# A transformer layer on one core: the same operations in another written-out order, with VectorE's additions of the means to the query weights set between operations of GpSimd

## The chip, the core and the metric

The kernel runs on one core of a Trainium2 chip. The metric is the device time of one execution in microseconds (us). The core has five engines that run their own instruction streams and wait for each other by semaphores: TensorE (PE in the profile, with its weight loads as PEld), VectorE (DVE), ScalarE (ACT), GpSimd (POOL) and SyncE (SP), which here only issues DMAs.

## The reference

One layer over 2048 rows of width 640: a linear attention of 32 heads of 20, then a gated product of two projections, both behind a layer norm and with a residual.

```python
def _A_ref(x, wqkv, w_phi, wo):
    qkv = (x @ wqkv) ...                      # q, k, v: 32 heads of 20
    pq = einsum("bhsd,hdf->bhsf", q, w_phi)
    pk = einsum("bhsd,hdf->bhsf", k, w_phi)
    phi_q = concatenate([softmax(pq), softmax(-pq)], axis=-1)
    phi_k = concatenate([softmax(pk), softmax(-pk)], axis=-1)
    kv = einsum("bhsf,bhsd->bhfd", phi_k, v)
    z  = einsum("bhsf->bhf", phi_k)
    num = einsum("bhqf,bhfd->bhqd", phi_q, kv)
    den = einsum("bhqf,bhf->bhq", phi_q, z) + 1e-6
    return (num / den) @ wo

def _B_ref(x, w_gate, w_up, w_down):
    return ((x @ w_gate) * (x @ w_up)) @ w_down

h = x + _A_ref(layernorm(x), A_wqkv, A_w_phi, A_wo)
h2 = h + _B_ref(layernorm(h), B_w_gate, B_w_up, B_w_down)
```

## The kernel before

The rows are worked on as 16 tiles of 128 (number T below), the widths as 5 chunks of 128. The layer norm's scale is applied behind the projections, its mean is folded into the weights, and w_phi is folded into the key and query weights, so that one projection gives the scores. Every step is recorded as an operation that belongs to a named unit; a unit may have operations on several engines:

- warm, wk, x0 to x4, wv, c0 to c4, wm, y0 to y4: preparation of the weights. x and y are rounds of TensorE that fold w_phi into the key and query weights, each evacuated by ScalarE (even numbers) or VectorE (odd). wk, wv and wm hold the sums over the weights; c subtracts the means from the value weights.
- **wq0 to wq4** (lines 744 to 755): add the mean (negative, nmeanq) to one chunk of the turned query weights, in place, 128x640 bf16. wq1 and wq3 are on ScalarE (L751), wq0, wq2 and wq4 on VectorE (L754, a tensor_scalar from SBUF to SBUF). Rounds y need all five.
- s0, s2, s4, s8, s12: layer norm statistics of two or four tiles: matmuls, a few reads by VectorE (L620, L624), then a chain of small operations on GpSimd that ends in the scales rs and nrs and, when there is time, the means mv (L640).
- **kT** (keys): a projection (10 matmuls of 320 columns; L579 is the helper that issues all matmuls), the largest absolute score by VectorE (L847), its product with the scale, called nb (L850), and two exponentials on ScalarE (L855) that read the projection's PSUM buffer. **KT** normalises them: sums (L869) and their reciprocals (L871) on VectorE, then one product over 128x1280 on GpSimd (L872).
- vT (values): a projection and one scaled copy by ScalarE (L878).
- **qT, QT** (queries): as kT and KT, with the sums at L909 and the reciprocals at L915 on VectorE, two products on GpSimd (L916, L921), and two transposing DMAs (L476).
- A0 to A14: the attention sums over two tiles each, one operation for each of two PSUM banks, 10 and 12 matmuls of 63 columns. A14 needs the last K. Aout: VectorE reads each bank with two operations (L959, L962) into KV. Everything after it needs KV.
- nT (numerator over denominator), hT (output projection, residual, statistics, turned by DMA or TensorE), fB.F.J (gate and up product of chunk F for four-tile block B), dT and eT (down projection and output).
- in, l..., t...: loads and transposing loads on SP. lx0 to lx3 each load four tiles of x.

There are 4 PSUM buffers of two banks (pool p_ps), 3 for the exponentials of queries, 2 each for the small sums and reciprocals. A unit that takes a buffer waits for whoever read it last. A projection holds its buffer until ScalarE's last exponential or copy of it.

The order of the operations on each engine is written out in the table ORDER: for each engine a list of units, where each mention takes the unit's next operation on that engine. `place()` walks through these lists, gives out the buffers, and `finish()` sets the semaphore waits. So an edit of ORDER moves operations, and with them the choice of buffers and the waits, but adds and removes no work.

```python
g.op("DVE", lambda e, a=a: e.tensor_scalar(out=WT[:, 0, a, :], in0=WT[:, 0, a, :], scalar1=nmeanq[:, a:a + 1], scalar2=None,
                                           op0=ALU.add), t=0.34, lat=0.46, rd=[R_nmu, R_WT[0][a]], wr=[R_WT[0][a]])
...
g.op("POOL", lambda e: e.tensor_tensor(out=x, in0=x, in1=Rk[:, vr.i, :].unsqueeze(2).to_broadcast([P, 2 * H, DH]), op=ALU.mult),
     rd=vr.R + R_phik[t], wr=R_phik[t], use=[vr], t=2.33)
```

The t and lat in the code are the author's estimates for the planner.

Of the kernel before, what the change touches and what calls it, by code (L numbers as in the profile page):

```python
# [61 lines left out]

ORDER = {
# [14 lines left out]
    "DVE":  # L78
# [11 lines left out]
    "ACT":  # L90
# [9 lines left out]
    "POOL":  # L100
# [10 lines left out]
}  # L111

# [1059 lines left out]
```

## Time and profile before

| | us |
|---|---|
| three runs | 280.05, 280.16, 280.05; median 280.05 |
| the profiled execution | 279.95 |
| its span, first to last instruction | 278.0 |
| granted clock of TensorE | 1.00 |
| first matmul; start of the last one | 0.8; 275.0 |

The profile is of one execution. In a timeline a row is: start, duration, engine, line, operation, output and inputs by the program's names (buffer numbers left out), size, count of merged instructions, and in brackets the idle time before it with what ended it. Matmul ends are modelled; the next run of matmuls starts a little before the modelled end of the last. By name, ps is PSUM, phik holds the key exponentials and later the product of gate and up, Phi later holds KV, phiqT holds the query weights at first (Wnat, WT) and later the turned query exponentials.

### The profile page before, as it was taken

Reading aid. Unit: us, or ns where it says so; the run is one execution under the profiler, and the core shown is the slowest. Engines: PE = TensorE matmul, PEld = TensorE weight load, DVE = VectorE, ACT = ScalarE, POOL = GpSimd, SP = SyncE. Lnnn points to the kernel's source line nnn. Section 1 sums busy time; section 2 is a strip of 40 time slices with the busy share of each in tenths; the row PEclk is TensorE's granted clock in tenths of the full one; section 3 lists DMA queues with packets and bytes.
Section 4 is the critical chain, followed back from the end, with each engine's and each line's share of the span. In section 5 each row is a group of like instructions: output and inputs, shape, how many; then the busy total and the mean of one; then the engine's idle time right before and its main releaser. Section 6 shows DMA issues by size and latency. Waiting matters only on the chain.

```text
span 278.0 us, 5602 instructions
## 1 busy us (share of the span) xinstructions
PE 272.8 (98%) x2271; PEld 185.3 (67%) x2271; DVE 167.8 (60%) x314; ACT 140.8 (51%) x249; POOL 107.7 (39%) x152
## 2 busy tenths in 40 slices
PE   8999999999899999999999999999999999999996
PEld 8877677778778888877744556554566444457773
DVE  1999999999999887787737637353400123142012
ACT  3468989999576945445267344324114232131330
POOL 5527989899832404034440401502305110000430
PEclk9999999999999999999999999999999999999999
DMA  8998899106176889738660165505111000001112
GB/s 197 276 144 211 124 320 400 66 2 96 30 91 120 173 246 189 149 72 120 127 129 2 36 133 74 106 2 118 47 26 47 0 26 0 0 0 50 47 48 72
DMA packets 67241, 28.60 MB, mean 103 GB/s; under 512 B 57744, under 2 KB 65936, under 8 KB 67216
## 3 DMA queue, kind: packets, MB, share of 16 engines
q1 hardware_dynamic: 66288, 27.90, 45.2%
q10 hardware_dynamic: 928, 0.35, 0.5%
q8 instruction: 18, 0.29, 0.5%
q14 instruction: 7, 0.06, 0.1%
HBM read 11.82 MB, written 2.62 MB: 52 GB/s over the span
## 4 chain that ended last, share of the span: by engine, by line
PE 88%; DVE 7%; DMA 2%; SPq 1%; issue 1%; ACT 1%
PE ps L579 87%; DVE Ssum L869 2%; DMA Wp<-in_A_wqkv_dram 2%; DVE ps L847 1%; DVE Sq L909 1%; SPq L476 1%; DVE Rk L871 1%; ACT phik L855 1%; DVE phiqT L754 1%; PE ps L487 0%; DVE outb L1077 0%; SPq L472 0%; DVE t L624 0%; DVE Phi L959 0%; DVE rq L915 0%
## 5 line engine op out<-in xcount | busy, mean ns | idle before, releaser
L579 PE MATMUL ps<-phik,Wgu 128*128 128x512 bf16 (+1 forms) x600 | 107.8, 336 | 0.0
L579 PEld LDWEIGHTS ps<-phik,Wgu 128*128 128x128 bf16 x600 | 58.1, 98 | 42.5 <-DVE phik L1036 0.6
L1036 DVE TENSOR_TENSOR phik<-ps,gate 128x512 bf16<-128x512 f32 (+1 forms) x60 | 34.4, 581 | 62.2 <-PE ps L579 60.3
L579 PE MATMUL ps<-Wp,xT 128*128 128x320 bf16 (+1 forms) x480 | 69.3, 299 | 0.5 <-ACT phik L855 0.5
L1034 ACT ACTIVATE gate<-ps 128x512 bf16<-128x512 f32 (+1 forms) x60 | 30.3, 511 | 63.5 <-PE ps L579 50.8
L579 PE MATMUL ps<-vaug,phik 128*128 128x320 bf16 (+3 forms) x560 | 59.3, 265 | 0.0
L579 PEld LDWEIGHTS ps<-Wp,xT 128*128 128x128 bf16 x480 | 45.7, 98 | 18.2 <-ACT phik L855 0.7
L579 PEld LDWEIGHTS ps<-vaug,phik 128*128 128x128 bf16 x560 | 42.8, 98 | 16.4 <-DVE phik L1036 0.2
L1052 POOL TENSOR_TENSOR outb<-t,x_all 128x640 bf16<-128x640 f32 x12 | 16.8, 1397 | 70.5 <-ACT t L1049 55.4
L872 POOL TENSOR_TENSOR phik<-phik,Rk 128x1280 bf16<-128x1280 bf16 x16 | 37.7, 2366 | 4.6 <-DVE Rk L871 4.3
L1049 ACT ACTIVATE t<-ps,mh,rs 128x640 f32<-128x640 f32 x12 | 10.6, 883 | 33.4 <-PE ps L579 33.4
L847 DVE TENSOR_REDUCE ps<-ps 128x1 f32<-128x640 f32 (+1 forms) x32 | 26.4, 826 | 1.8 <-PE ps L579 1.4
L909 DVE TENSOR_REDUCE Sq<-eq 128x66 f32<-128x1320 bf16 x16 | 24.1, 1513 | 1.4 <-ACT eq L855 1.4
L869 DVE TENSOR_REDUCE Ssum<-phik 128x64 f32<-128x1280 bf16 x16 | 23.6, 1473 | 0.1
L916 POOL TENSOR_TENSOR rq<-Sq,rq 128x33 f32<-128x33 f32 x16 | 4.1, 255 | 46.4 <-DVE rq L915 42.4
L921 POOL TENSOR_TENSOR eq<-eq,rq 128x660 bf16<-128x660 bf16 x16 | 20.9, 1305 | 1.0
L855 ACT ACTIVATE eq<-ps,nb,rs 128x300 bf16<-128x300 f32 (+2 forms) x26 | 17.0, 688 | 6.1 <-DVE nb L850 5.9
L572 ACT ACTIVATE junk<-x_all 128x640 bf16<-128x640 bf16 x20 | 14.8, 738 | 9.5 <-DVE x_all L1013 9.4
L855 ACT ACTIVATE eq<-ps,nb,nrs 128x300 bf16<-128x300 f32 (+2 forms) x26 | 17.3, 692 | 0.0
L855 ACT ACTIVATE phik<-ps,nb,rs 128x640 bf16<-128x640 f32 x16 | 14.3, 891 | 3.2 <-DVE nb L850 3.0
L1013 DVE SCALAR_TENSOR_TENSOR x_all<-ps,mh,x_all 128x640 bf16<-128x640 f32 x16 | 14.1, 883 | 0.7
L855 ACT ACTIVATE phik<-ps,nb,nrs 128x640 bf16<-128x640 f32 x16 | 14.3, 896 | 0.0
(86 smaller groups left out, 225.0 us busy)
## 6 DMA issues: line engine op xcount, KB each, us to landing
x_all<-in_A_x_dram SPq DMA_DIRECT2D x4, 640.0 KB, 4.8
out_dram<-outb SPq DMA_DIRECT2D x15, 160.0 KB, 1.8
Wgu<-in_B_w_gate_dram SPq DMA_DIRECT2D x1, 1920.0 KB, 10.5
Wgu<-in_B_w_up_dram SPq DMA_DIRECT2D x1, 1920.0 KB, 16.0
vaug<-in_B_w_down_dram SPq DMA_DIRECT2D x1, 1920.0 KB, 9.6
Wp<-in_A_wqkv_dram SPq DMA_DIRECT2D x1, 800.0 KB, 5.0
phiqT<-in_A_wqkv_dram SPq DMA_DIRECT2D x1, 800.0 KB, 6.5
Wo<-in_A_wo_dram SPq DMA_DIRECT2D x1, 800.0 KB, 6.2
```

The source lines that it names most:

```text
L572: g.op("ACT", lambda e: e.activation(out=junk[:, v.i, :], in_=in_, func=func, accum_out=acc), rd=rd, wr=wr, use=[v], t=0.73, lat=0.97)
L579: ins = e.matmul(o_, lhsT=l_, rhs=r_, start=s_, stop=p_, skip_group_check=True)
L847: g.op("DVE", lambda e: e.tensor_reduce(out=mx(), in_=src(), axis=AX.XY if len(src().shape) == 3 else AX.X, op=ALU.max, apply_absolute_val ...
L855: g.op("ACT", lambda e, s=s, sc=sc, to=to, of=of: e.activation(out=to(s), in_=of(), func=ACT.Exp, bias=nb[:, i:i + 1], scale=sc[:, t:t + 1 ...
L869: g.op("DVE", lambda e: e.tensor_reduce(out=Ssum[:, vs.i, :], in_=x, axis=AX.X, op=ALU.add), rd=R_phik[t], wr=vs.R, use=[vs], t=1.39, lat=1.5)
L872: g.op("POOL", lambda e: e.tensor_tensor(out=x, in0=x, in1=Rk[:, vr.i, :].unsqueeze(2).to_broadcast([P, 2 * H, DH]), op=ALU.mult), rd=vr.R ...
L909: g.op("DVE", lambda e: e.tensor_reduce(out=Sq[:, vs.i, :].rearrange("p (w g) -> p w g", w=NQ), in_=feat(0, NQ).rearrange("p w (g f) -> p ...
L921: return e.tensor_tensor(out=x, in0=x, in1=rq[:, vr.i, :].rearrange("p (w h) -> p w h", h=HW).unsqueeze(3).to_broadcast([P, NQ, HW, DH]), ...
L1013: g.op("DVE", lambda e: e.scalar_tensor_tensor(out=xv, in0=PS[v.i][:, :, 0:HALF], scalar=mh[:, t:t + 1], in1=xv, op0=ALU.subtract, op1=ALU ...
L1034: g.op("ACT", lambda e: e.activation(out=gate[:, vg.i, 0:P * n], in_=PS[v.i][:, 0, 0:P * n], func=ACT.Copy), rd=[v.R[0]], wr=vg.R, use=[v, ...
L1036: g.op("DVE", lambda e: e.tensor_tensor(out=hhT[:, hb, ft, sl], in0=PS[v.i][:, 1, 0:P * n], in1=gate[:, vg.i, 0:P * n], op=ALU.mult), rd=[ ...
L1052: g.op("POOL", lambda e: e.tensor_tensor(out=outb[:, vo.i, :], in0=t32[:, v3.i, :], in1=x_all[:, t, :], op=ALU.add), rd=v3.R + [R_h[t]], w ...
```

## The change

Only the table ORDER differs; the operations, their sizes and their operands are the same. On VectorE wq4 moves from behind the sum of K3 to behind the reciprocal of K0, wq2 from behind the max of k7 to behind the max of k2, and wq0 stays behind the nb of k7, which now has K3's reciprocal ahead of it. Around them keys, values and queries change places on all engines: on TensorE v2 goes ahead of k2 and v0 between the matmuls of s4, q2 and q3 go ahead of most of A, and the last of A stands as A14, A12, A14. On VectorE k8's max goes ahead of k11's nb. The units of the second half are ordered anew as well. The diff, cut after the parts that go up to the attention sums and the first rows behind them:

```diff
--- before.py
+++ after.py
@@ -62,51 +62,50 @@
 
 ORDER = {
     "PE":
-        "warm wk wk wk wk wk wk wk wk wk wk s0 s0 x1 x1 x3 wv wv x2 x0 x0 s2 s2 x4 k0 k0 k0 k0 k0 k3 k1 wm k2 v0 v2 s4 s4 s4 s4 "
-        "k7 v3 k4 v7 y2 k6 y3 v5 y1 v4 k5 y0 s8 s8 s8 s8 v1 y4 k10 q0 s12 s12 s12 s12 k11 k9 k8 v6 v13 q1 v11 k12 v9 k13 v10 "
-        "v12 k14 v8 k15 v15 A0 A2 A4 A0 A2 q2 A6 A4 A8 q3 A10 q5 v14 A6 A8 A10 A12 A12 A14 A14 n0 n1 n1 n0 q7 n1 q4 n0 h1 h0 n2 "
-        "q6 h1 h0 n3 q8 f0.0.0 f0.0.0 f0.10.0 f0.10.0 f0.4.0 f0.4.0 h2 f0.5.0 f0.5.0 h3 f0.8.0 f0.6.0 f0.8.0 f0.6.0 f0.1.0 q10 "
-        "f0.9.0 f0.2.0 f0.1.0 f0.9.0 f0.2.0 f0.2.2 f0.2.2 f0.1.2 n7 f0.4.2 f0.1.2 f0.4.2 f0.11.2 f0.11.2 f0.7.0 n5 q9 f0.7.0 "
...
+        "warm wk wk wk wk wk wk wk wk wk wk s0 s0 x1 x1 x3 wv wv x2 x0 x0 s2 s2 x4 k0 k0 k0 k0 k0 k3 k1 wm v2 k2 s4 v0 s4 s4 s4 "
+        "k7 v3 k4 v7 y2 k6 y3 v5 y1 v4 k5 y0 s8 s8 s8 s8 v1 y4 k10 q0 s12 s12 s12 s12 k11 k8 k9 v6 v13 q1 v9 k12 v11 k13 v10 "
+        "k14 v15 v12 k15 v8 q2 A0 A0 A2 q3 A4 A6 A2 v14 A4 q5 A8 A6 A10 A12 A8 A10 A14 A12 A14 n1 n0 n1 n0 q7 n1 q4 n0 h1 h0 n2 "
+        "q6 h1 h0 n3 q8 f0.10.0 f0.10.0 f0.0.0 f0.0.0 f0.4.0 f0.4.0 h2 f0.5.0 f0.5.0 h3 f0.6.0 f0.6.0 f0.1.0 f0.1.0 q10 f0.8.0 "
+        "f0.9.0 f0.8.0 f0.9.0 f0.2.0 f0.2.0 f0.2.2 f0.2.2 f0.4.2 n7 f0.11.2 f0.4.2 f0.11.2 n5 q9 f0.10.2 f0.10.2 f0.7.0 f0.7.0 "
...
     "DVE":
-        "wk in in in wk wk wk s0 wk s0 s0 x1 x3 c4 c3 s2 s2 c1 c0 k0 s2 k0 c2 k3 k1 k3 K0 k1 k2 K0 K3 wq4 K3 k2 s4 s4 s4 s4 s4 "
-        "K1 k7 wq2 k7 wq0 K2 k4 K1 k4 K2 k6 y3 K4 y1 K4 k6 K7 k5 s8 s8 s8 s8 s8 k5 K6 K7 k10 K6 k10 q0 s12 K5 q0 k11 K5 k11 K10 "
-        "k8 k9 k8 K11 k9 Q0 K11 K10 q1 Q0 q1 K9 k12 K9 k12 K8 Q1 k13 K8 k13 K12 k14 Q1 K12 k14 K13 k15 K13 k15 K14 q2 K14 q2 "
-        "K15 q3 K15 q3 Q2 q5 Q2 Q3 Aout Aout Aout Q3 Aout n0 n1 q5 n1 n1 n0 n1 n0 n0 Q5 q7 Q5 q7 q4 h1 h1 h0 q4 h0 n2 n2 Q7 n3 "
...
+        "wk in in in wk wk wk s0 wk s0 s0 x1 x3 c1 c0 c3 s2 s2 c4 k0 s2 k0 c2 k3 k1 k3 K0 K0 wq4 k1 K3 k2 wq2 k2 s4 s4 s4 s4 s4 "
+        "K1 k7 K3 k7 wq0 K2 k4 K2 k4 K1 k6 y3 K4 y1 K4 k6 K7 k5 s8 s8 s8 s8 k5 s8 K7 K6 k10 K6 k10 q0 s12 K5 q0 k11 K5 k8 k11 "
+        "K10 k9 k8 K11 k9 Q0 K11 q1 K10 K9 K8 q1 K9 k12 k13 K8 Q0 k12 Q1 k14 k13 K12 k14 Q1 K12 K13 k15 K13 k15 K14 q2 K14 q2 "
+        "K15 q3 K15 q3 Q2 Q2 q5 Q3 Aout Aout Q3 Aout Aout n1 q5 n0 n1 n1 n0 n1 n0 n0 q7 Q5 q7 Q5 q4 h1 q4 h1 h0 h0 n2 n2 Q7 n3 "
...
     "ACT":
-        "in in in wk wk wk x2 x0 x4 k0 k0 wm k3 k3 k1 k1 v0 v2 k2 wq3 k2 wq1 v3 k7 k7 v7 y2 k4 k4 s12 v5 s12 v4 s12 y0 k6 k6 y4 "
-        "k5 k5 v1 s12 k10 k10 q0 q0 k11 k11 v6 k8 v13 k8 k9 k9 v11 q1 q1 wo4 v9 wo0 v10 k12 k12 v12 k13 k13 v8 wo1 k14 k14 wo3 "
-        "k15 v15 k15 wo2 q2 wo0 q2 q3 q3 v14 wo3 wo4 wo2 wo1 q5 q5 n1 n0 q7 q7 q4 q4 q4 q4 h0 h1 f0.0.0 f0.10.0 f0.4.0 q6 q6 q6 "
...
+        "in in in wk wk wk x2 x0 x4 k0 k0 wm k3 k3 v2 k1 k1 v0 k2 k2 wq3 wq1 v3 k7 k7 v7 y2 k4 k4 s12 v5 s12 v4 s12 y0 k6 k6 k5 "
+        "y4 k5 v1 k10 s12 k10 q0 q0 k11 k11 v6 k8 k8 k9 k9 v13 v9 wo0 wo4 v11 q1 q1 v10 k12 k12 v15 k13 k13 k14 v12 k14 wo3 v8 "
+        "k15 k15 wo1 q2 q2 v14 q3 q3 wo1 wo4 q5 q5 wo3 wo2 wo0 n1 wo2 n0 q7 q7 q4 q4 q4 q4 h1 h0 f0.10.0 f0.0.0 f0.4.0 q6 q6 q6 "
...
     "POOL":
-        "in in in in in in in in in in in in pad in in pad wk s0 in s0 s0 s0 in s0 s2 s0 s2 s2 s2 s2 s2 K0 s4 s4 s4 s4 s4 s4 K3 "
-        "s0 K1 K2 K4 s8 s8 s8 s8 s8 s8 K7 s12 s12 K6 in s12 s12 in s12 K5 s12 K11 K10 Q0 K9 Q0 K8 Q1 Q1 K12 K13 K14 K15 Q2 Q2 "
-        "s8 Q3 Q3 s4 Q5 Q5 s2 Q7 Q7 h1 h2 Q4 Q4 h1 h2 Q6 Q6 Q8 Q8 Q9 Q9 Q10 h0 h0 Q10 d1 h3 h7 Q12 Q12 d2 s12 Q11 Q11 h8 h8 h3 "
-        "h7 Q13 h4 Q14 Q13 h6 Q14 h11 Q15 Q15 d0 h4 h9 h5 h6 h10 h12 d3 h13 h5 h13 h11 h9 h12 d4 h10 d7 d6 d5 h15 h15 d9 d11 "
...
+        "in in in in in in in in in in in in pad in in pad wk s0 in s0 s0 s0 s0 s2 s0 s2 s2 s2 s2 s2 K0 s4 s4 s4 s4 s4 s4 K3 in "
+        "K2 K1 K4 in s8 s8 s8 s8 s8 s8 K7 K6 s12 s12 K5 in s12 s12 s12 s12 s4 s8 s0 K11 K10 K9 Q0 K8 Q0 Q1 Q1 K12 K13 K14 K15 "
+        "Q2 Q2 Q3 Q3 s2 Q5 Q5 s12 Q7 Q7 Q4 Q4 h1 h1 Q6 Q6 h3 h0 Q10 Q8 Q10 h3 Q8 h0 h2 h2 Q9 Q9 h5 Q12 Q12 d2 d1 h4 Q11 Q11 h8 "
+        "Q14 Q14 h7 d3 Q13 Q15 Q13 Q15 h6 h6 h4 d0 h9 h7 h10 h10 h11 d4 h5 h14 h14 h8 h11 h12 h12 h13 h13 d7 d6 h9 d5 h15 h15 "
...
     "SP":
-        "Q1 Q0 Q2 Q2 Q3 Q3 Q5 Q5 n2 n3 Q7 Q7 lx1 h2 h3 Q4 Q4 ld n7 Q6 Q6 Q8 lx2 Q8 n5 n4 n6 Q9 Q9 h7 Q10 h4 Q10 n8 d1 h5 h6 n9 "
-        "n10 Q12 Q12 Q11 Q11 n11 Q13 n12 Q13 Q14 h8 h9 Q14 h11 h10 n13 Q15 Q15 n14 n15 h13 d2 d0 h12 d3 h14 h15 d4 d7 d5 e12 d6 "
+        "Q1 lx2 Q0 Q2 Q2 Q3 Q3 Q5 Q5 n2 n3 Q7 Q7 h2 h3 Q4 Q4 lx1 n7 Q6 Q6 n5 ld n4 Q8 Q8 Q10 n6 Q10 h5 n8 Q9 h4 Q9 h6 h7 h8 Q12 "
+        "Q12 n9 n10 d2 d1 Q11 Q11 n12 Q14 Q14 n11 n14 Q13 h9 h11 h10 Q15 Q13 d3 Q15 h12 n13 h14 n15 h13 h15 d4 d0 d7 d6 d5 e12 "
 }
```

43 rows, old and new, of the table ORDER are left out of this document.

## The prediction

> **What bounds the kernel now.** I read the page first, then the busy time by stretch, then what TensorE waits for, then the timelines of the engines around each of those waits.
>
> ```profile
> span 278.0 us, 5602 instructions
> ...
> PE 272.8 (98%) x2271; PEld 185.3 (67%) x2271; DVE 167.8 (60%) x314; ACT 140.8 (51%) x249; POOL 107.7 (39%) x152
> ```
> ```profile
> 9.00:29.00 20.00, 19.37 (x201) 14.70 (x198) 19.49 (x43) 13.82 (x20) 10.55 (x21) 1.00 0.98 191
> 29.00:75.00 46.00, 45.35 (x517) 34.58 (x518) 45.11 (x79) 41.81 (x69) 42.97 (x37) 1.00 0.54 150
> 75.00:85.00 10.00, 9.63 (x115) 7.23 (x113) 9.72 (x25) 7.26 (x11) 3.50 (x6) 1.00 0.69 99
> 85.00:270.00 185.00, 185.00 (x1300) 117.84 (x1298) 88.61 (x156) 74.13 (x146) 45.49 (x67) 1.00 0.37 76
> ```
> ```profile
> PE ps L579 <- DVE Phi L962: 0.9, 2, 0.6
> ...
> PE ps L579 <- ACT phik L855: 0.5, 1, 0.5
> ```
>
> The columns of the second fence are length, then PE, PEld, DVE, ACT, POOL, clock, DMA share. From 85 to 270 us TensorE is busy 185.00 of 185.00 us: there an order can only lose. All that it can win lies ahead of 85 us. There VectorE is full too (19.49 of 20 us, 45.11 of 46 us) and GpSimd nearly (42.97 of 46). The matmuls are the same in both kernels, so the time changes by TensorE's waits alone. The page counts idle time by modelled ends; I measure a wait from start to start. First the wait at 29 us, with VectorE, GpSimd and ScalarE before it:
>
> ```profile
> 21.46 1.30 PE L579 MATMUL ps<-xT 128*128 128x129 bf16 x20
> ...
> 28.03 0.48 PE L579 MATMUL ps<-Phi,phiqT 128*128 128x140 bf16 x6
> 29.01 1.53 PE L579 MATMUL ps<-Wp,xT 128*128 128x320 bf16 x10 [0.51 <-ACT phik L855]
> 30.38 0.48 PE L579 MATMUL ps<-Phi,phiqT 128*128 128x140 bf16 x6
> 30.70 0.57 PE L579 MATMUL ps<-Wp,xT 128*128 128x320 bf16 x3
> ```
> ```profile
> 17.77 1.48 DVE L869 TENSOR_REDUCE Ssum<-phik 128x64 f32<-128x1280 bf16 x1
> ...
> 21.76 1.36 DVE L754 TENSOR_SCALAR phiqT<-phiqT,nmeanq 128x640 bf16<-128x640 bf16 x1
> 23.05 0.54 DVE L871 RECIPROCAL Rk<-Ssum 128x64 f32<-128x64 f32 x1
> ...
> 23.52 0.15 DVE L620 COPY sm<-ps 128x4 f32<-128x4 f32 x1
> ...
> 24.43 1.48 DVE L869 TENSOR_REDUCE Ssum<-phik 128x64 f32<-128x1280 bf16 x1
> 25.83 0.82 DVE L847 TENSOR_REDUCE ps<-ps 128x1 f32<-128x640 f32 x1
> 26.56 0.37 DVE L754 TENSOR_SCALAR phiqT<-phiqT,nmeanq 128x640 bf16<-128x640 bf16 x1
> 26.85 0.14 DVE L850 TENSOR_TENSOR nb<-ps,rs 128x1 f32<-128x1 f32 x1
> 26.92 0.37 DVE L754 TENSOR_SCALAR phiqT<-phiqT,nmeanq 128x640 bf16<-128x640 bf16 x1
> ```
> ```profile
> 20.58 2.36 POOL L872 TENSOR_TENSOR phik<-phik,Rk 128x1280 bf16<-128x1280 bf16 x1 [3.28 <-DVE Rk L871]
> ...
> 26.99 2.51 POOL L872 TENSOR_TENSOR phik<-phik,Rk 128x1280 bf16<-128x1280 bf16 x1
> ```
> ```profile
> 23.63 0.88 ACT L855 ACTIVATE phik<-ps,nb,rs 128x640 bf16<-128x640 f32 x1 [1.16 <-DVE nb L850]
> ...
> 27.30 0.88 ACT L855 ACTIVATE phik<-ps,nb,rs 128x640 bf16<-128x640 f32 x1
> 28.07 0.89 ACT L855 ACTIVATE phik<-ps,nb,nrs 128x640 bf16<-128x640 f32 x1
> ```
>
> Round y3 starts at 30.38 and the next projection 0.32 later; y2 starts at 28.03, so k6 could have started at 28.35. It started at 29.01: **a wait of 0.66**, for the second exponential of k7 (28.07 + 0.89 = 28.96). Behind it stands wq4: 1.36 us where its two sisters took 0.37, because it began at 21.76 inside GpSimd's K0 (20.58 to 22.94) and ended 0.18 after it. Next, the waits after the attention sums A, with VectorE's rows:
>
> ```profile
> 71.83 2.33 PE L579 MATMUL ps<-vaug,phik 128*128 128x63 bf16 x74
> 74.80 0.49 PE L579 MATMUL ps<-Phi,phiqT 128*128 128x63 bf16 x10 [0.64 <-DVE Phi L962]
> 75.55 0.53 PE L579 MATMUL ps<-Phi,phiqT 128*128 128x42 bf16 x12 [0.26 <-DVE Phi L962]
> ...
> 79.24 2.91 PE L579 MATMUL ps<-Wo,phik 128*128 128x320 bf16 x20
> 82.25 0.49 PE L579 MATMUL ps<-Phi,phiqT 128*128 128x63 bf16 x11
> ```
> ```profile
> 66.46 0.85 DVE L847 TENSOR_REDUCE ps<-ps 128x1 f32<-128x660 f32 x1 [0.50 <-PE ps L579]
> ...
> 72.77 1.47 DVE L909 TENSOR_REDUCE Sq<-eq 128x66 f32<-128x1320 bf16 x1
> 74.16 0.45 DVE L959 TENSOR_TENSOR Phi<-ps,Gk 128x300 bf16<-128x300 f32 x1
> ```
>
> A run of matmuls hands over about 0.16 before its modelled end (29.01 + 1.53 against 30.38). So TensorE was free at 74.00, 75.12 and 81.99 and started at 74.80, 75.55 and 82.25: **waits of 0.80, 0.43 and 0.26**. With the 0.66 that is 2.15 us, the most that this stretch can give back.
>
> **The change part by part.** The profiled execution took 279.95 us, 1.95 outside its span; the three runs shown have the median 280.05, 0.10 more. I work in the trace's clock and put the difference on 280.05.
>
> *wq4 behind the reciprocal of K0.* K0's sum now comes ahead of k1's nb, then its reciprocal, then wq4. Sum 17.77 + 1.48, 0.04 to the dependent reciprocal: 19.29. A reciprocal takes 0.46 to the next start (23.05, one small operation, 23.52): wq4 at 19.75. GpSimd's K0 starts 0.08 after the reciprocal's end (19.83), at 19.91. wq4 is first by 0.16 and should take 0.37 (0.29 to the next start, 26.56 to 26.85). K0 loses some 0.15 to it, as the 2.51 against 2.36 at 26.99 shows, where wq0 was ahead by 0.07. Then k1's nb at 20.04, K3's sum 20.11 (1.40 to the next start, 24.43 to 25.83), k2's max 21.51 (0.73 to 0.75), wq2 22.26, as K0 ends (22.4 to 22.5), k2's nb 22.55. The price of wq2 lies between 0.37 and 0.6; I take 0.37.
>
> *What this gives.* k1's nb is 0.9 later than before, covered by v2 and k2, which TensorE now has ahead. s4's matmuls end at 21.46 + 1.30 = 22.76, and their first reader started at 23.52; now VectorE waits for them and starts at 22.80. From there to k7's max the operations are the same: 25.83 - 0.72 = 25.11. Then 0.73 and K3's reciprocal 0.46: k7's nb 26.30, its end 26.4. ScalarE starts k2 right after its nb, 22.75 instead of 23.63, and has the same five operations up to k7: 22.75 + 27.30 - 23.63 = 26.42. So k7's second exponential ends at 26.43 + 0.77 + 0.89 = 28.09, and k6 starts at 28.35 with 0.2 to spare: **0.66 gained** (bounds 0 and 0.66). wq0 starts with the end of K3's reciprocal, some 0.1 ahead of GpSimd's K3.
>
> *What is late next: v13.* In the new DVE order k8's max stands ahead of k11's nb.
>
> ```profile
> 44.68 0.09 DVE L850 TENSOR_TENSOR nb<-ps,rs 128x1 f32<-128x1 f32 x1
> ```
> ```profile
> 45.19 0.88 ACT L855 ACTIVATE phik<-ps,nb,rs 128x640 bf16<-128x640 f32 x1
> 45.96 0.89 ACT L855 ACTIVATE phik<-ps,nb,nrs 128x640 bf16<-128x640 f32 x1
> ```
> ```profile
> 41.50 7.79 PE L579 MATMUL ps<-Wp,xT 128*128 128x320 bf16 x56
> ```
>
> In the old clock nb moves from 44.68 to 45.41 and is over at 45.56; k11's first exponential goes from 45.19 to 45.59, the second ends at 47.25 instead of 46.85. v13 writes the PSUM buffer that k11 holds. It is the fifth projection from 41.50, due at 46.94 (1.36 each). VectorE, which waits for q0 just before, cannot get ahead of TensorE to cover it. **0.37 lost** (bounds 0 and 0.6). Between there and A, k14, v12 and q2 also get their buffers within 0.1 us of need by the same walk: **0.10 lost** (0 to 0.5).
>
> *The attention sums.* A14 for bank 0 now stands ahead of A12 and A14 for bank 1 (before, both of A12 stood ahead of it), so it starts 0.93 before TensorE runs out instead of 0.64, and ends 0.47 before. From VectorE's first of the two reads to the next matmul it took 74.80 - 74.16 = 0.64. VectorE was the late one before: it came out of a 1.47 us sum at 74.16. Now it loses neither the 0.50 at 66.46 (q2 stands ahead of all of A) nor the 0.66 of the front; a few tenths come back because nb costs 0.07 behind anything but a reciprocal. It arrives at 73.2 to 73.4. TensorE is out of work at 74.00 - 0.66 + 0.37 + 0.10 = 73.81 and the reads can start at 73.81 - 0.43 = 73.38: the two meet. The wait is 0.21 instead of 0.80. The second stays 0.43 to 0.45, since the reciprocal of Q3 only changes places with a read. **0.57 gained** (0.25 to 0.8). For n2 (0.26) I count nothing: q7's nb now stands behind Q5's sum (-0.3 to +0.26).
>
> *The rest.* GpSimd's last memsets and the tiny mv operations move ahead of K7 and K11, into the 3 us of 46 that it has free there. Among SP's moves lx2, a load of four tiles, goes between the transposes of Q1 and Q0; all of A, which reads neither, covers the delay of one issue, and if the load slowed them by more than A lasts, n0 would wait for the rest. From 85 us on, each matmul group that I walked keeps at least the buffer distance of before: 0, at most 0.4 lost.
>
> Sum: 0.66 - 0.37 - 0.10 + 0.57 = 0.76 gained; 280.05 - 0.76 = **279.29, say 279.3**.
>
> **The shared port.** Row: 1.36 against 0.37, and 2.51 against 2.36. The Trainium skill (SBUF — State Buffer, § SBUF: two separate sides) says that VectorE in a two-port mode and GpSimd take one port pair as an exclusive lock: whoever starts first keeps it for its whole instruction and the other blocks. By that rule, the trace agrees in both directions, and the same rule speaks against this change: it sets wq4 and wq0 at the very point where GpSimd is released, so that a race decides.
>
> **The rivals.**
> 1. *GpSimd wins the race at K0* (slower). If K0 starts ahead of wq4, wq4 ends 0.18 after it, at 19.91 + 2.36 + 0.18 = 22.45 instead of 20.12. k1's exponentials then end near 24.1, and k7, which needs their buffer, starts at 24.2 instead of 22.59; VectorE, 2.33 behind the walk above and so 1.6 behind the old kernel, has only the 0.50 and part of the 0.57 to recover: 280.05 + 1.3 = 281.3. It decides if the lead of 0.16 is gone. Against it: a lead of 0.07 sufficed at 26.92. Chance 0.10.
> 2. *The gain is handed back ahead of A.* If the margins under 0.1 (k6, y4, k14, v12, q2) each fail by 0.1 to 0.2, or VectorE reaches A at 73.8, some 0.2 to 0.4 remain: 279.65 to 279.9. For it: VectorE 45.11 of 46. Chance 0.22.
> 3. *New waits after 85 us.* With 185.00 of 185.00 busy any miss costs in full; two to four misses of 0.3 give 279.9 to 280.6. Against it: VectorE and ScalarE are under half busy. Chance 0.08.
>
> **How the numbers follow.** The forecast has 0.60 and by itself runs from 278.8 to 279.7. About 0.2% (0.56 us) is what a measurement can tell from no change, so the line is 279.49. Faster: 0.49 of the forecast and 0.05 of rival 2, 0.54. Same: 0.11 + 0.14 + 0.02 = 0.27. Slower: 0.03 + 0.10 + 0.06 = 0.19. The range 278.7 to 280.8 leaves out rival 1 and little tails.
>
> **What would show it.** wq4, wq2 and wq0 at 0.37 each; k6 without a wait at 28.3; a wait of 0.3 to 0.4 at v13; the first matmul after A 0.7 earlier than 74.80, with 0.2 waited; nothing after 85 us. A wq of 1 us or more, or a wait of TensorE at k7, is rival 1; idle TensorE between 50 and 73 us is rival 2. I am wrong if k11's nb does not delay v13, or if VectorE is over 0.3 late at A.

## The result and the profile after

The changed kernel takes **279.44 us** (median of 15 runs, 279.12 to 279.72), the kernel before 280.05 (15 runs beside it, 279.84 to 280.36). The ratio is 0.9976 with a 95% interval of 0.9969 to 0.9984, which is 0.45 to 0.87 us less. Forecast were 279.3 and a gain of 0.76; the medians differ by 0.61. The profiled execution took 279.5 with a span of 277.6.

The line numbers after are one less than before (the table ORDER is one line shorter). The profile after lacks 13 matmul records, so busy shares are not compared; waits are measured from start to start as in the prediction, with 0.16 taken off the modelled end of the run of matmuls ahead. First VectorE and GpSimd around the query weights (timeline of the changed kernel: start, duration, engine, line, operation):

```profile
18.02 1.48 DVE L868 TENSOR_REDUCE Ssum<-phik 128x64 f32<-128x1280 bf16 x1
19.52 0.55 DVE L870 RECIPROCAL Rk<-Ssum 128x64 f32<-128x64 f32 x1
19.99 0.29 DVE L753 TENSOR_SCALAR phiqT<-phiqT,nmeanq 128x640 bf16<-128x640 bf16 x1
...
22.39 0.38 DVE L753 TENSOR_SCALAR phiqT<-phiqT,nmeanq 128x640 bf16<-128x640 bf16 x1
...
26.56 0.38 DVE L753 TENSOR_SCALAR phiqT<-phiqT,nmeanq 128x640 bf16<-128x640 bf16 x1
```
```profile
20.16 2.36 POOL L871 TENSOR_TENSOR phik<-phik,Rk 128x1280 bf16<-128x1280 bf16 x1 [2.62 <-DVE Rk L870]
...
26.71 2.43 POOL L871 TENSOR_TENSOR phik<-phik,Rk 128x1280 bf16<-128x1280 bf16 x1 [0.28 <-DVE nb L849]
```

wq4 starts 0.17 ahead of K0 and takes 0.29 instead of 1.36; wq2 and wq0 take 0.38. Now TensorE at the places of the old waits and the new ones (timeline of the changed kernel, five windows):

```profile
28.27 0.48 PE L578 MATMUL ps<-Phi,phiqT 128*128 128x140 bf16 x6
28.59 1.52 PE L578 MATMUL ps<-Wp,xT 128*128 128x320 bf16 x10
```
```profile
43.78 2.88 PE L578 MATMUL ps<-Wp,xT 128*128 128x320 bf16 x20
46.82 2.37 PE L578 MATMUL ps<-Wp,xT 128*128 128x320 bf16 x16 [0.16 <-ACT phik L854]
```
```profile
71.32 2.74 PE L578 MATMUL ps<-vaug,phik 128*128 128x63 bf16 x88
74.13 0.49 PE L578 MATMUL ps<-Phi,phiqT 128*128 128x63 bf16 x10
74.88 0.53 PE L578 MATMUL ps<-Phi,phiqT 128*128 128x42 bf16 x12 [0.26 <-DVE Phi L961]
```
```profile
83.02 0.72 PE L486 MATMUL ps<-ident,x_all 128*128 128x128 bf16 x10
83.86 0.49 PE L578 MATMUL ps<-Phi,phiqT 128*128 128x63 bf16 x11
```
```profile
120.77 2.08 PE L578 MATMUL ps<-Wo,vaug 128*128 128x320 bf16 x14
122.88 0.51 PE L578 MATMUL ps<-Phi,phiqT 128*128 128x63 bf16 x11
```

k6 starts at 28.59, 0.32 behind y2: its wait of 0.66 is gone. v13 was due at 43.78 + 2.88 - 0.16 = 46.50 and starts at 46.82: a new wait of 0.32. Behind the attention sums TensorE was free at 73.90 and starts at 74.13 (0.23 instead of 0.80), then again at 74.88 (0.42 as before). The 0.26 ahead of n2 is gone, but n3, due at 83.58, waits 0.28. And n8, due at 122.69, waits 0.19, where the kernel before had nothing. The sum is 0.66 - 0.32 + 0.57 + 0.01 + 0.26 - 0.28 - 0.19 = **0.71 gained**.

The last matmul, though, starts only 0.46 earlier (the kernel before, then the changed one):

```profile
275.02 0.22 PE L579 MATMUL ps<-vaug,phik 128*128 128x128 bf16 x1
```
```profile
274.56 0.22 PE L578 MATMUL ps<-vaug,phik 128*128 128x128 bf16 x1
```

The rest is at the very start, where the order of the two kernels is still the same (again before, then after):

```profile
9.40 0.45 PE L579 MATMUL ps<-Wp,ones 128*128 128x320 bf16 x2
```
```profile
9.65 0.45 PE L578 MATMUL ps<-Wp,ones 128*128 128x320 bf16 x2 [0.31 <-DMA Wp<-in_A_wqkv_dram]
```

This is the first matmul that needs the load of the weights (unit wv). It starts at 9.65 after, at 9.40 before. In the profiles of the experiments below it starts anywhere from 9.40 to 10.16, and in two of them (the first and the fifth) the order up to there is that of the kernel before: 9.51 and 9.89. So its place differs from execution to execution and is no effect of the change. The clean measure of a trace is therefore the **distance from the start of wv to the start of the last matmul**: 265.62 before, 264.92 after, 0.70 less, in line with the sum of the waits.

### The profile page after: what moved, and what is told of

It reads as the page before. It is cut to its first block, busy times and chain, and to the rows that moved or that the text cites. A ratio compares the mean times of both kernels' runs of the same rounds, so it can differ in the third digit from the quotient of the medians.

```text
span 277.6 us, 5581 instructions
## 1 busy us (share of the span) xinstructions
PE 272.1 (98%) x2258; PEld 185.0 (67%) x2271; DVE 167.3 (60%) x314; ACT 141.6 (51%) x249; POOL 107.8 (39%) x152
## 4 chain that ended last, share of the span: by engine, by line
PE 83%; DVE 7%; POOL 4%; DMA 2%; issue 1%; SPq 1%
PE ps L578 82%; POOL phik L871 3%; DVE ps L846 2%; DMA Wp<-in_A_wqkv_dram 2%; DVE Sq L908 2%; DVE Ssum L868 2%; POOL eq L920 1%; SPq L475 1%; DVE Rk L870 1%; PE ps L486 0%; DVE outb L1076 0%; SPq L471 0%; DVE Phi L958 0%; DVE rq L914 0%; DVE nb L849 0%
## 5 line engine op out<-in xcount | busy, mean ns | idle before, releaser
L578 PE MATMUL ps<-phik,Wgu 128*128 128x512 bf16 (+1 forms) x588 | 106.0, 335 | 0.5
L1069 DVE SCALAR_TENSOR_TENSOR outb<-ps,rs,t 128x640 bf16<-128x640 f32 x3 | 2.7, 884 | 20.8 <-PE ps L578 18.0
L1018 POOL TENSOR_SCALAR vpe<-shc 128x1 f32<-128x1 f32 x16 | 3.1, 191 | 30.3 <-ACT junk L571 29.4
```

The lines of the kernel that those rows point to most:

```text
L578: ins = e.matmul(o_, lhsT=l_, rhs=r_, start=s_, stop=p_, skip_group_check=True)
```

## The experiments

Each is timed beside the kernel before on its chip, whose medians there were 280.12 to 280.16. "Distance" is the measure just named, of the profiled execution.

| kernel | median us (runs) | ratio, 95% interval | distance us |
|---|---|---|---|
| before | 280.05 (15) | 1 | 265.62 |
| changed | 279.44 (15) | 0.9976 (0.9969 to 0.9984) | 264.92 |
| 1 before, wq4 moved alone | 279.62 (12) | 0.9997 (0.9975 to 1.0018) | 264.95 |
| 2 changed, wq4 put back | 279.92 (11) | 0.9994 (0.9985 to 1.0002) | 265.46 |
| 3 changed, nb of k11 first | 279.49 (11) | 0.9977 (0.9968 to 0.9986) | 264.88 |
| 4 changed, old end of A | 279.72 (11) | 0.9984 (0.9975 to 0.9992) | 265.47 |
| 5 before, new end of A | 280.25 (12) | 1.0000 (0.9988 to 1.0011) | 265.62 |
| 6 changed, lost race | 281.29 (12) | 1.0036 (1.0025 to 1.0048) | 267.06 |
| 7 changed, nb of q12 earlier | 279.26 (8) | 0.9959 (0.9944 to 0.9974) | 265.13 |
| 8 changed, 3 and 7 together | 279.17 (10) | 0.9959 (0.9946 to 0.9972) | 264.94 |
| 9 changed, ld earlier | 279.77 (11) | 0.9992 (0.9983 to 1.0001) | 265.15 |
| 10 changed, three repairs | 279.37 (8) | 0.9965 (0.9938 to 0.9993) | 264.92 |
| 11 changed, again | 279.41 (12) | 0.9973 (0.9964 to 0.9983) | 264.89 |
| 12 changed, three repairs, other place of ld | 278.94 (5) | 0.9957 (0.9943 to 0.9971) | 264.46 |

**1. wq4 alone, in the kernel before.**

```diff
-  K0 K3 wq4 K3 k2 s4
+  K0 wq4 K3 K3 k2 s4
```

> The kernel before, with nothing changed but wq4 moved ahead of the sum of K3, so that it follows the reciprocal of K0. Theory of the prediction: the place of wq4 alone sets the wait of k6. wq4 should start about 20.5, ahead of GpSimd's K0, and take 0.3 to 0.4 instead of 1.36; VectorE is then some 0.9 earlier, k6 starts without its wait of 0.66, and the waits behind A stay as before (0.80, 0.43): 279.2 to 279.5. First rival (the gain needs the exchange of keys, values and queries around it, or is handed back ahead of A): 279.75 to 280.1. Second rival (GpSimd's K0 gets the port first): wq4 over 2 us, above 280.5.

VectorE and TensorE of this kernel:

```profile
20.07 0.54 DVE L871 RECIPROCAL Rk<-Ssum 128x64 f32<-128x64 f32 x1
20.53 0.29 DVE L754 TENSOR_SCALAR phiqT<-phiqT,nmeanq 128x640 bf16<-128x640 bf16 x1
```
```profile
28.14 0.48 PE L579 MATMUL ps<-Phi,phiqT 128*128 128x140 bf16 x6
28.45 1.52 PE L579 MATMUL ps<-Wp,xT 128*128 128x320 bf16 x10
...
71.81 1.78 PE L579 MATMUL ps<-vaug,phik 128*128 128x63 bf16 x55
74.22 0.49 PE L579 MATMUL ps<-Phi,phiqT 128*128 128x63 bf16 x10 [0.64 <-DVE Phi L962]
```

wq4 takes 0.29, k6 starts 0.31 behind y2 without a wait, and the wait behind A is 0.79 as before (free at 73.43). The distance falls by 0.67, just the old wait of k6. By the median the kernel is 0.54 faster than the 280.16 beside it; two of its twelve runs, at 281.24 and 283.12, make the ratio's interval too wide to say so by itself, and 279.62 lies 0.12 above the expected range. The mechanism is shown by the trace: the place of one operation of 0.3 us sets that wait, and none of the exchanges around it is needed. The distance of this kernel, 264.95, is also that of the changed kernel to 0.03: all the other exchanges together gain next to nothing, for the 0.57 behind A goes again in the new waits of v13 (0.32) and n8 (0.19).

**2. wq4 put back, in the changed kernel.**

```diff
-  K0 K0 wq4 k1 K3 k2
+  K0 K0 k1 K3 wq4 k2
```

> The changed kernel with wq4 alone put back behind the sum of K3, so that it starts inside GpSimd's K0 again. Theory: wq4 starts near 21.5, takes about 1.2 and ends 0.2 behind K0; VectorE is 0.9 later from there, k6 waits 0.6 to 0.8 again, and the time is 280.0 to 280.4. Rival (the new order around it has enough cover, so the place of wq4 does not matter): 279.3 to 279.6.

```profile
21.47 1.30 DVE L753 TENSOR_SCALAR phiqT<-phiqT,nmeanq 128x640 bf16<-128x640 bf16 x1
```
```profile
28.34 0.48 PE L578 MATMUL ps<-Phi,phiqT 128*128 128x140 bf16 x6
29.28 1.40 PE L578 MATMUL ps<-Wp,xT 128*128 128x320 bf16 x9 [0.46 <-ACT phik L854]
```

GpSimd's K0 ran from 20.23 to 22.59 and wq4 ended at 22.77, 0.18 behind it, as in the kernel before. The wait of k6 is back with 0.62. The time is 279.92, just below the expected range. The distance grows by 0.54: the 0.62 of k6, less 0.10 at n8. The wait behind A stays at 0.24. VectorE does not make up there what it lost; its first read behind A, in the changed kernel and then in this one, comes 0.71 later (0.06 of it is wv):

```profile
73.48 0.46 DVE L958 TENSOR_TENSOR Phi<-ps,Gk 128x300 bf16<-128x300 f32 x1
```
```profile
74.19 0.46 DVE L958 TENSOR_TENSOR Phi<-ps,Gk 128x300 bf16<-128x300 f32 x1
```

But TensorE is later by the same, 0.69 at k6, so the two still meet.

**3. The nb of k11 ahead of the max of k8.**

```diff
-  q0 k11 K5 k8 k11 K10 k9 k8
+  q0 k11 K5 k11 k8 K10 k9 k8
```

> The changed kernel with the nb of k11 ahead of the max of k8 again, as in the kernel before. Theory: the wait of 0.33 ahead of v13 comes from this exchange alone; without it 279.1 (0.33 less). Rival (the max of k8, now later by 0.1 and its nb behind it, only moves the wait to k9's or k8's buffers, or VectorE is the late one at A anyway and the wait returns there): 279.3 to 279.5.

TensorE, in two windows that begin on either side of the start of k14:

```profile
56.48 1.78 PE L578 MATMUL ps<-Wp,xT 128*128 128x320 bf16 x10
```
```profile
56.86 1.40 PE L578 MATMUL ps<-Wp,xT 128*128 128x320 bf16 x9
```

No wait is left ahead of v13, so the exchange did cause it. But two matmuls that lie 0.14 apart elsewhere are 0.38 apart here: k14 waits 0.25 for the buffer of q1, which in the changed kernel came free 0.10 ahead of need. TensorE is 0.33 earlier and VectorE is not, for q1's nb stands behind K8's sum. The distance is 264.88 against 264.92. The rival holds: the wait only moved, to another buffer than the rival named.

**4. The old end of A, in the changed kernel, and 5. the new end, in the kernel before.**

```diff
-  A8 A10 A14 A12 A14
+  A8 A10 A12 A14 A14
```

> The changed kernel with the last matmuls of the attention sums as before (both of A12 ahead of A14). Theory: VectorE, free at 73.5, now waits for A14 of bank 0, which ends 0.3 later, so the wait ahead of n1 is 0.5 to 0.55 instead of 0.24 and the second stays at 0.4: 279.7. Rival (the gain behind A is VectorE's earlier arrival alone, and the order of A14 and A12 counts for nothing): 279.4.

```diff
-  A10 A12 A12 A14 A14
+  A10 A12 A14 A12 A14
```

> The kernel before with nothing changed but the last matmuls of the attention sums, in the new order A14, A12, A14. Theory: VectorE was the late one there (it left a sum of 1.47 at 74.16, 0.4 behind the end of A14 of bank 0), so an earlier A14 gives nothing: 280.0 to 280.1, and the waits stay 0.80 and 0.43. Rival (the order of the matmuls makes the gain behind A): 279.5 to 279.75.

VectorE and TensorE at the end of A, first of the changed kernel with the old end, then of the kernel before with the new end:

```profile
73.74 0.47 DVE L958 TENSOR_TENSOR Phi<-ps,Gk 128x300 bf16<-128x300 f32 x1 [0.18 <-PE ps L578]
```
```profile
74.40 0.49 PE L578 MATMUL ps<-Phi,phiqT 128*128 128x63 bf16 x10 [0.35 <-DVE Phi L961]
```
```profile
73.25 1.47 DVE L909 TENSOR_REDUCE Sq<-eq 128x66 f32<-128x1320 bf16 x1
74.64 0.45 DVE L959 TENSOR_TENSOR Phi<-ps,Gk 128x300 bf16<-128x300 f32 x1
```
```profile
72.13 2.50 PE L579 MATMUL ps<-vaug,phik 128*128 128x63 bf16 x80
75.28 0.49 PE L579 MATMUL ps<-Phi,phiqT 128*128 128x63 bf16 x10 [0.64 <-DVE Phi L962]
```

With the old end VectorE now idles 0.18 for TensorE, and the wait is 0.50 instead of 0.23 (free at 73.90); 279.72 was expected and measured to 0.02. Of the 0.55 that the distance grows, this wait is 0.27, a wait in the opening (at 12.33) 0.16, and n8, with 0.31, 0.12. In the kernel before the new end changes nothing: VectorE comes out of its sum at 74.64 with no idle time, the wait is 0.81, the distance the same to 0.01 (the median, 280.25, lies 0.15 above the expected range). So **the gain behind A needs both**, an earlier VectorE and an earlier A14: VectorE alone gives 0.30 of the 0.57, the order the other 0.27, and the order alone nothing. Earlier means against TensorE: in experiment 1 both come 0.6 earlier (73.58 against 74.16 and 73.43 against 74.00), and the wait stays. What brings VectorE ahead of TensorE was read from the traces, and no run undoes it alone: q2's projection stands ahead of A now, and the idle 0.50 that VectorE had ahead of q2's max (66.46 in the kernel before) is gone. The row of the changed kernel has no bracket:

```profile
65.68 0.84 DVE L846 TENSOR_REDUCE ps<-ps 128x1 f32<-128x660 f32 x1
```

**6. The lost race.**

```diff
-  K0 K0 wq4 k1 K3 k2 wq2 k2
+  K0 K0 wq4 wq2 k1 K3 k2 k2
```

> The changed kernel with wq2 directly behind wq4, so that it is issued at about 20.2, at the point where GpSimd's K0 begins (20.16). If whoever starts first keeps the port for its whole instruction and K0 has it: wq2 lasts until 0.2 after K0's end, some 2.4 us, the nb of k1 comes 2.3 later, k7 waits for a buffer, and the time is 280.8 to 281.6, the first rival of the prediction. If the two share the port (a slowdown by the factor that wq4 showed in the kernel before, 1.36 to 0.37): wq2 takes 1.0 to 1.4 and the time is 279.8 to 280.5. If VectorE keeps the port from wq4 to wq2: wq2 takes 0.3 to 0.4, K0 some 0.2 to 0.3 longer than its 2.36, and the time stays 279.4 to 279.6.

VectorE (a window that holds wq2 alone), GpSimd and TensorE:

```profile
20.09 2.50 DVE L753 TENSOR_SCALAR phiqT<-phiqT,nmeanq 128x640 bf16<-128x640 bf16 x1
```
```profile
20.05 2.36 POOL L871 TENSOR_TENSOR phik<-phik,Rk 128x1280 bf16<-128x1280 bf16 x1 [2.61 <-DVE Rk L870]
```
```profile
21.88 1.01 PE L578 MATMUL ps<-xT 128*128 128x129 bf16 x15
24.42 1.80 PE L578 MATMUL ps<-Wp,xT 128*128 128x320 bf16 x12 [1.52 <-ACT phik L854]
```

wq2 starts 0.04 behind K0 and takes 2.50, to 0.18 behind K0's end; K0 takes its usual 2.36. k7 waits 1.69 for a buffer, and the time is 281.29, where the first rival of the prediction, with wq4 as the loser in place of wq2, was priced at 281.3. Sharing would have given wq2 1.0 to 1.4. The Trainium skill (SBUF — State Buffer, § SBUF: two separate sides) calls the pair of ports an exclusive lock that whoever starts first keeps for the whole instruction; the trace agrees, with 2.50 here and 1.30 for an operation that started 1.24 behind K0's start (experiment 2), both ending 0.18 behind K0. With VectorE first GpSimd loses less than such a lock would take, the whole overlap: K0 overlaps the last 0.12 of wq4 in the changed kernel and takes its usual 2.36, K3 overlaps 0.23 of wq0 and takes 2.43, and in the kernel before it overlaps 0.30 and takes 2.51.

**7 and 8. The nb of q12.** What waits at 122.88? n8 writes the PSUM buffer that the exponentials of q12 read last, and their nb stood behind the first read of n6.

```diff
-  f0.7.2 f0.6.2 f0.9.2 f0.11.0 n6 q12 n6
+  f0.7.2 q12 f0.6.2 f0.9.2 f0.11.0 n6 n6
```

> The changed kernel with one small operation of VectorE, the nb of q12, moved four places ahead, so that it no longer stands behind the first read of n6. Theory: the wait of 0.18 ahead of n8 at 122.88 is for q12's last exponential, which that nb holds up; without it 279.25. Rival (behind 85 us another buffer is late at once): 279.45.

ScalarE of the changed kernel, then of this one:

```profile
119.27 0.38 ACT L1033 ACTIVATE gate<-ps 128x256 bf16<-128x256 f32 x1 [0.59 <-PE ps L578]
120.65 1.14 ACT L854 ACTIVATE eq<-ps,nb,rs 128x300 bf16<-128x300 f32 x2 [1.00 <-DMA phiqT<-eq]
```
```profile
119.15 0.38 ACT L1033 ACTIVATE gate<-ps 128x256 bf16<-128x256 f32 x1 [0.59 <-PE ps L578]
120.75 1.15 ACT L854 ACTIVATE eq<-ps,nb,rs 128x300 bf16<-128x300 f32 x2 [1.21 <-DMA phiqT<-eq]
```

The theory falls: with the nb long done (at 116.34), the exponentials still start at 120.75, and the wait of n8 is 0.40. The bracket names the cause, in the changed kernel too: they wait for a DMA, a transpose out of the buffer eq that they are to overwrite. (The median of this kernel, 279.26, is below that of the changed kernel on other chips, while its trace is 0.21 longer; medians of 8 to 12 runs on different chips don't settle differences of 0.2.)

> The changed kernel with both repairs: the nb of k11 ahead of the max of k8, and the nb of q12 ahead of the first read of n6. Theory: the two waits of 0.33 and 0.18 are independent and both go: 278.9 to 279.0, better than both kernels. Rival (VectorE becomes late at A, or the second wait returns): 279.1 to 279.4.

The trace has the 0.25 of k14 in place of the 0.32 of v13, and n8 waits 0.24: distance 264.94, no gain over the changed kernel. The median, 279.17, lies in the rival's range.

**9, 10 and 11. The load of w_down.** The DMA out of eq is that of Q8. Its landing (DMAs of the changed kernel issued between 113 and 115, median time to landing) against all of its kind (page of the profile, part 6):

```profile
phiqT<-eq SPq DMA_TRANSPOSE x2, 6.0
```
```profile
phiqT<-eq SPq DMA_TRANSPOSE x32, 2.8
```

They run beside ld, a load of 1920 KB, issued at 108.14 and 9.1 us on its way. The change had moved ld behind the transposes of n7, Q6 and n5. Putting it back:

```diff
-  lx1 n7 Q6 Q6 n5 ld n4 Q8 Q8
+  lx1 ld n7 Q6 Q6 n5 n4 Q8 Q8
```

> The changed kernel with one DMA moved on SP: ld, the load of w_down, ahead of the transposes of n7, Q6 and n5, as in the kernel before. Theory, formed after the last runs: the wait ahead of n8 does not come from the nb of q12 but from the transposes of Q8, which were issued while ld was running (5.6 to 6.4 us to landing, others 2.5 to 2.9) and hold the buffer that q12's exponentials write. With ld earlier they should land in 2.5 to 3.5 us, q12's exponentials start right behind ScalarE's product at 119.7 instead of 120.65, and the wait of 0.2 to 0.4 ahead of n8 goes: 0.2 less than the changed kernel on the same chip. Rival (ld, now nearer to lx1, slows the transposes of n7, Q6 or n5, and another matmul waits for them instead): as the changed kernel or slower.

TensorE and ScalarE of this kernel:

```profile
112.32 0.71 PE L578 MATMUL ps<-phik,Wgu 128*128 128x256 bf16 x5
113.27 0.94 PE L578 MATMUL ps<-phik,Wgu 128*128 128x256 bf16 x7 [0.23 <-ACT eq L854]
```
```profile
111.03 1.15 ACT L854 ACTIVATE eq<-ps,nb,rs 128x300 bf16<-128x300 f32 x2 [0.92 <-DVE rden L993]
```

The wait ahead of n8 is gone, so ld was its cause (the second of Q8's transposes still takes 4.65, but lands at 119.07). But now Q6's transposes take 5.5 and 6.3 to land, the last at 110.92; q9's exponentials start at 111.03 and f0.8.2 waits 0.40 for them. (The bracket names VectorE, which ended its read 0.06 before the exponential's start; that operation is no input of it.) The trace is 0.26 longer than that of the changed kernel run beside it, the median 0.36 higher: the rival. With k11 and q1 repaired as well:

```diff
-  K11 q1 K10 K9 K8 q1 K9 k12
+  K11 q1 K10 K9 q1 K8 K9 k12
```

> The changed kernel with three repairs: the nb of k11 ahead of the max of k8; the nb of q1 ahead of the sum of K8, because the first repair only moved the wait to k14, which needs the buffer of q1 (0.25 at 56.3); and ld as in the run beside it. Theory: the three waits of 0.33, 0.25 and 0.2 are all gone and none is added ahead of A: 0.5 less than the changed kernel on the same chip, 278.9 to 279.0, better than both kernels. Rival (VectorE is full ahead of A, so the 0.33 come back as a longer wait ahead of n1): 0.2 less only.

The waits at v13 and k14 are gone, and nothing came back ahead of A (n1 waits 0.16). But f0.8.2 now waits 0.46, and the distance is that of the changed kernel; 279.37 is far from the expected 278.9 to 279.0, and not for the reason that the rival named.

> The changed kernel itself, as the measure for the two others on this chip: 279.4 to 279.5, with the waits that its first profile showed (0.33 ahead of v13, 0.24 and 0.42 behind A, 0.28 ahead of n3, 0.1 to 0.3 ahead of n8). The wait of wv near 9.6 for the load of the weights should differ from the first profile's, as it did between all the runs so far (the matmul started between 9.4 and 10.2), since nothing ahead of it is changed.

279.41, with the waits 0.33, 0.24, 0.43 and 0.17 at the same places and the distance the same to 0.03; only the 0.28 of n3 is now 0.12 at n2 and 0.15 at n3. wv started at 9.56.

**12. ld between Q6 and n5.** As 10, but ld stands only one place earlier than in the changed kernel.

```diff
-  lx1 n7 Q6 Q6 n5 ld n4 Q8 Q8
+  lx1 n7 Q6 Q6 ld n5 n4 Q8 Q8
```

> As the run with three repairs, but ld stands only one DMA earlier than in the changed kernel: behind the transposes of Q6, which slowed down beside it (5.5 to 6.8 us to landing, q9's exponentials waited for them and f0.8.2 for those, 0.40 to 0.46), and ahead of those of n5. Theory: ld then runs from about 106.5 to 116, Q6 lands ahead of 109, Q8 ahead of 119, and neither n8 nor f0.8.2 waits; with the waits ahead of v13 and k14 gone too, 0.6 less than the changed kernel: 278.8 to 279.0. Rival (any place of ld between 98 and 117 slows some transposes that a matmul needs): a wait of 0.2 to 0.5 stays and the time is 279.1 to 279.4.

TensorE of this kernel at n8, and the windows view (length, then PE, PEld, DVE, ACT, POOL, clock, DMA share):

```profile
121.74 0.85 PE L578 MATMUL ps<-Wo,vaug 128*128 128x321 bf16 x5
122.42 0.50 PE L578 MATMUL ps<-Phi,phiqT 128*128 128x63 bf16 x11
```
```profile
29.00:75.00 46.00, 45.71 (x532) 34.63 (x530) 45.55 (x85) 41.05 (x65) 44.21 (x41) 1.00 0.59 166
```

n8 starts where the run ahead ends (122.43), and neither f0.8.2, v13 nor k14 waits. It is close: Q8's transposes still take 5.6 and 4.1 and land by 119.92, not ahead of 119 as expected, and q12's last exponential ends only 0.2 before n8 starts. **278.94** (278.84 to 279.15): the fastest of all, 0.46 less distance than the changed kernel. VectorE is busy 45.55 of 46 us in that stretch; TensorE's waits left there are 0.07 at v12 and, behind A, 0.16 and 0.45. The intervals of the two ratios still overlap; that it beats the kernel before is clear (0.9943 to 0.9971), that it beats the changed kernel rests on the traces and the medians of different chips.

## Why the prediction was right, step by step

- **wq4.** Right. The start was walked to 19.75 and K0's to 19.91; the trace has 19.99 and 20.16, later by the 0.25 that wv was late in that execution. k7's second exponential, walked to 28.09, ends at 28.36. It took 0.29 and not 0.37, wq2 and wq0 0.38, and K0 lost nothing to it (2.36) where I gave it 0.15. The lead over K0 is 0.17 in all eleven profiles in which wq4 stands right behind the reciprocal: both follow that same reciprocal, and the race came out the same way each time.
- **k6, 0.66 gained.** Right, and shown by undoing it (0.62 back) and by doing it alone (0.67).
- **v13, 0.37 lost.** Right in place and cause; 0.32 measured. I did not see that without it k14 would be late.
- **k14, v12 and q2, 0.10 lost.** Measured nothing: the buffers came free 0.10, 0.17 and 0.06 ahead of the start, and none of the three waited.
- **The attention sums, 0.57 gained.** Right: 0.80 to 0.23, where 0.21 was forecast. That the two late ones "meet" is shown from both sides by experiments 4 and 5.
- **n2, nothing counted.** The sum is right (0.26 gone, 0.28 new at n3), but by luck, for the wait was read wrongly. In the kernel before, n2 takes the PSUM buffer of h1, and VectorE's residual of h1 ends last, at 82.10:

```profile
81.22 0.88 DVE L1013 SCALAR_TENSOR_TENSOR x_all<-ps,mh,x_all 128x640 bf16<-128x640 f32 x1
```

  The exponentials of q7, whose nb the forecast names, hold the buffer that q6 takes. In the changed kernel n2 takes the buffer of q7, free at 81.10, and does not wait; n3 then waits for VectorE's reading of n2, which ends at 83.71 and stands behind the residual of h0.
- **From 85 us on, 0, at most 0.4.** Here a step failed: I walked buffer distances of TensorE's groups and, of SP's moves, weighed only lx2. ld, which slowed the transposes that stand behind it, is a move on the same queue. It cost 0.19 (0.17 in the second profile, and 0.09 to 0.40 over all eight profiles with ld at that place).

The trace's sum is 0.71 against the forecast's 0.76: +0.05 at v13, +0.10 ahead of A and -0.19 at n8 nearly cancel, so that part of the agreement is luck. The medians give 0.61.

Of the rivals, the first did not come, and its price was about right (281.29 in experiment 6 against 281.3; that it fits to 0.01 is luck, for the distance there is 1.44 more than before where 1.3 was priced). The point from which it decides was right too: 0.17 of lead win, 0.04 the other way lose everything. The second did not come: v13 is the only wait of TensorE between 29 and 73 us. The third came with one miss of 0.19, smaller than the two to four misses of 0.3 that it was priced at.

## What to carry to other kernels

The short VectorE operation from SBUF to SBUF beside the long one of GpSimd cost either 0.3 us or all that was left of the other: set such an operation so that it is released clearly first, and price the lost race by the whole length of GpSimd's operation. A wait that is taken away is worth what the next margin behind it allows, so list the margins (here 0.10 at k14) before adding gains up. When an order of DMAs changes, ask of every large load which small transfers will run beside it, and who needs the buffer that they read.

## What the runs showed of the hardware that was not expected

- Transposing DMAs issued while a load of 1920 KB is on its way, and over 1 us before it lands, take 3.7 to 6.9 us to land (one, issued 0.6 behind the load, 9.5), at each of the three places of the load. With no load on its way (from 60 us on, all profiles) the median is 2.6, but about one in six takes 3.4 to 5.1 there too, and no run shows why. Moving the load chose which matmul waits, and only the third place found transposes that had that much time.
- The first matmul on the loaded weights started between 9.40 and 10.16 in executions whose order up to there is the same; how the loads land is a spread of some tenths of a us in every time above.
- The same tensor_scalar took 0.29 directly behind a reciprocal (in each of the kernels where it stood there) and 0.37 to 0.38 behind others; nb took 0.09 to 0.10 behind a reciprocal and 0.14 to 0.16 behind all else. The cause was not tried.
